# Attention read-out and three-way maxout on one Trainium2 core: two maxima apart, permuted state tokens, shared copies and new orders

## The chip, the cores and the metric

The kernel runs on one core of one Trainium2 chip, so there is no traffic between cores. The metric is the device time of one execution in microseconds (us). TensorE is called PE in the profile (its weight loads PEld), VectorE DVE, ScalarE ACT, GpSimd POOL and SyncE SP; ACT, POOL and SP also issue DMA transfers, each from its own queue.

## What is computed

There are 8 batches of 8 heads, 512 tokens and 32 state tokens per batch, and 64 numbers per head. The tokens read the states by softmax attention, and the states read the tokens. Both read-outs, 544 rows of 512 numbers per batch, then pass through three weight matrices at once; the largest of the three products is kept, and a fourth matrix gives the output.

```python
scores = scale * x @ state.T                  # 512 x 32 for a head
a = exp(scores - max); a /= a.sum(-1)
xread = a @ state                             # tokens read states
sread = softmax(scale * state @ x.T) @ x      # states read tokens
t = concatenate([xread, sread])               # 544 rows of 512 in a batch
h = maximum(maximum(t @ w1, t @ w2), t @ w3)  # 768 wide
out = h @ w_out                               # 512 wide, float32
```

## The kernel before

The kernel never forms xread. For each batch it multiplies the states into the weights first: G is state times w1, w2 and w3 (`g_slice` and `g_run`, matmuls of L326, copied out of PSUM at L344, L365 and L368). A token's row of t @ w is then its 256 attention weights times G.

A batch b passes through these steps. Each has a short name in the order strings.

- `lx`, `lxg`, `lxu` load x; `lw`, `lwo` load the weights, `lst` the states. `lw m0 m1 i` loads columns 128 m0 to 128 m1 of weight i, counted from 0. `stc`, `stt`, `stp` cast, transpose and place the states.
- `xt`/`xtc` (or `xtd`, a DMA transpose on SP's queue) give x transposed. `sc` makes the scores (L234), `ex` the exponentials on ACT (L241), `sum` their sums on DVE (L248, L250), `wt` the weights a (L256).
- `at`/`atc` (or `atd`, again a DMA transpose on SP's queue) give aT. `pad`, `sr`, `srs`, `srt` form sread and put it, transposed, into the tile `ats`.
- `g`/`gc` and `gr`/`grc` give G. Batches 0 and 1 take it in slices of 128 columns of each weight, later ones in runs of columns.
- `l1 b m` is layer 1 for slice m of the 768 columns: six matmuls of 512 columns into three PSUM banks `pw` (L378). `m0` copies the first bank to a bf16 tile t0 on ACT (L393). `m1` does two maxima on DVE, one behind the other: t1 = max(t0, second bank) at L399, and ht = max(t1, third bank) at L404.
- `l2 b j` is layer 2, six matmuls of 512 columns (L411), one for each slice m. `l2c` copies the result to the tile `osb` (L418), `so` stores it (L438).
- `l1s`, `l2 s`, `sos` do the same for the 256 state tokens of all batches at the end: twelve matmuls of 256 columns for a slice.

PSUM has four single banks (pool `pw`, which layer 1, layer 2, `sr`, the transposes and the short `gr` share) and two pairs of banks (pool `two`, for G and the scores). A matmul into a bank waits until the copy or maximum that read its last contents is done.

The order on every engine is written by hand, in three strings: FIRST (batches 0 and 1, and the start of 2), EACH (performed five times, b = 2 to 6, for layer 1 of batch b, the attention of batch b+1 and layer 2 of batch b-1) and LAST (layer 1 of batch 7, layer 2 of 6 and 7, the state tokens). `perform` (L491) walks through them, and each engine and each queue works off its part in that order. `busy n` issues n matmuls on zeros (L183), which compute nothing.

The end of the program checks sums and would branch to a slower form for other inputs; that branch doesn't run here.

Of the kernel before, what the change touches and what calls it, by code (L numbers as in the profile page):

```python
# [8 lines left out]
F32 = mybir.dt.float32  # L9
BF16 = mybir.dt.bfloat16  # L10
# [4 lines left out]


FIRST = """
    lxg 0 1; lst 1 S; lxu 0 0 A; lxg 1 0; ident; zero; busy 2; lw 0 2 1; lst 0 A; lxg 1 1; clr 0; clr 1;
    lw 0 3 0; busy 2; busy 1; busy 6; busy 1; lw 0 3 2; stc 0 P; stc 1 P; cxu 0 0 A; busy 1; busy 5; stt 0;
    busy 2; xt 0 0; busy 1; clr 3; warm; lw 2 6 1; stp 0 D; xt 0 1; xtc 0 1 D; lw 3 4 0; lw 3 4 2;  # L20
    xtc 0 0 A; xt 1 0; sc 0 0; xtc 1 0 D; ex 0 0; busy 1; sum 0 0; sc 0 1; xt 1 1; lx 2; ex 0 1; busy 2;
    sc 1 0; xtc 1 1 A; sum 0 1; stt 1; busy 2; xones 0; ex 1 0; wt 0 0 P; wt 0 1 P; sc 1 1; sum 1 0; busy 2;
    wt 1 0 P; sr 0; at 0 0; ex 1 1; at 0 1; xones 1; srs 0; stp 1 A; sum 1 1; g 0 0; wt 1 1 P; g 1 1;
    atc 0 1 A; atc 0 0 A; gc 0 0 D; sr 1; at 1 0; busy 1; srs 1; lw 4 6 2; g 0 1; g 1 0; gc 1 1 A; at 1 1;
    atc 1 1 A; gc 0 1 D; l1 0 0; g 0 2; gc 1 0 D; g 1 2; atc 1 0 A; m0 0 0; gc 0 2 A; l1 1 0; m0 1 0;
    gc 1 2 A; m1 0 0; l1 1 1; g 0 3; g 1 3; m0 1 1; m1 1 0; l1 0 1; m1 1 1; lw 4 6 0; m0 0 1; l1 0 2; xtd 2;
    l1 1 2; pad 2; m0 0 2; g 0 4; g 0 5; gc 0 3 A; gc 1 3 A; m0 1 2; gc 0 4 A; gc 0 5 A; clr 2; m1 0 1;
    l1 0 3; g 1 4; m0 0 3; lst 3 S; m1 0 2; gr 2 0 512; m1 1 2; grc 2 0 512 A; m1 0 3; l1 1 3; m0 1 3;
    sc 2 -; gc 1 4 A; l1 0 5; l1 1 4; m1 1 3; m0 0 5; lwo; l1 0 4; lst 2 S; gr 2 1024 1280; m1 0 5; g 1 5;
    m0 1 4; lx 3; ex 2 -; gr 2 1280 1792; xtd 3; m0 0 4; m1 1 4; sr 2; m1 0 4; grc 2 1024 1280 A; l2 0 2;  # L30
    sum 2 -; gc 1 5 D; l2 0 3; l2 0 0; gr 2 1792 2304; lx 4; wt 2 - P; l2c 0 3 D; stc 2 D;
    grc 2 1280 1792 A; srs 2; gr 2 512 1024; l2c 0 0 D; l2c 0 2 D; l1 1 5; m0 1 5; stt 2; grc 2 1792 2304 A;
    stc 3 P; grc 2 512 1024 A; l2 0 1; stt 3; m1 1 5; atd 2; l2c 0 1 D; stp 2 A; so 0 0 2 P; stp 3 D;
    so 0 2 4 P; ones;
"""
EACH = """
    sc 1 -; l2 -1 0; gr 1 1792 2304; gr 1 0 512; srt -2; ex 1 -; lx 3; grc 1 1792 2304 D; pad 1; l2 -1 3;
    l2c -1 0 D; l1 0 0; grc 1 0 512 A; l2 -1 1; m0 0 0; sum 1 -; l2c -1 3 A; gr 1 1024 1280; m1 0 0;
    gr 1 1280 1792; gr 1 512 1024; sr 1; grc 1 1024 1280 A; l1 0 1; l1 0 2; l2c -1 1 D; m0 0 1; srs 1;
    m0 0 2; l2 -1 2; m1 0 1; m1 0 2; grc 1 512 1024 A; l1 0 3; wt 1 - P; grc 1 1280 1792 D; m0 0 3; m1 0 3;  # L40
    l2c -1 2 A; l1 0 5; l1 0 4; xtd 2; so -1 0 2 P; m0 0 5; m0 0 4; m1 0 5; atd 1; m1 0 4; so -1 2 4 P;
"""
LAST = """
    srt 5; srt 6; l1 7 0; l2 6 2; l2 6 1; m0 7 0; l1 7 2; l2c 6 1 A; l1 7 3; l1 7 4; l2c 6 2 D; srt 7;
    m1 7 0; l1s 0; m0 7 2; m0 7 3; l1 7 1; l1 7 5; m0 7 4; m1 7 2; m0 s 0; l2 6 0; m0 7 1; m1 7 3; m1 7 4;
    l2 6 3; m1 s 0; l1s 2; l1s 1; m0 7 5; m1 7 1; m1 7 5; l2 7 0; l2 7 1; m0 s 2; l2c 6 0 D; l1s 3; look;
    m1 s 2; m0 s 1; l2p 7 2 0 256; l1s 5; l2c 6 3 D; l2c 7 0 D; m0 s 3; l2pc 7 2 0 256 A; so 6 0 2 A;
    sop 7 2 0 256 S; m1 s 1; l2c 7 1 D; m0 s 5; m1 s 3; l2p 7 2 256 512; m1 s 5; l1s 4; m0 s 4;
    l2pc 7 2 256 512 D; m1 s 4; l2 s 0; l2c s 0 D; flag; l2 7 3; sos 0 S; l2c 7 3 D; sop 7 2 256 512 S;
    so 7 3 4 S; l2 s 1; so 6 2 4 A; l2c s 1 A; so 7 0 2 P; sos 1 A;  # L50
"""


# [1 line left out]
def kernel(  # L55
# [10 lines left out]
    nc = tc.nc  # L66

    B, H, S, D = x.shape
    _, _, Ns, _ = state.shape
# [3 lines left out]
    d_model, d_ff = moe_w1.shape  # L73
# [3 lines left out]
    J = 4  # L77
    HS = H // 2
# [5 lines left out]
    data = ctx.enter_context(tc.tile_pool(name="data", bufs=1))  # L84
    work = ctx.enter_context(tc.tile_pool(name="work", bufs=2))
# [4 lines left out]
    copier = {"D": nc.vector.tensor_copy, "A": nc.scalar.copy, "P": nc.gpsimd.tensor_copy}  # L90
# [10 lines left out]
    x_f = {}  # L101
    w_sb = data.tile([128, HS, 3, d_ff], BF16, name="w")
    wout_sb = data.tile([128, NM, d_model], BF16, name="wout")
    zero = const.tile([128, 512], BF16, name="zero")
    ident = const.tile([128, 128], BF16, name="ident")
    ones = const.tile([128, 128], BF16, name="ones")
    warm = const.tile([128, 1], F32, name="warm")
    ats = data.tile([128, B, HS, Ns], BF16, name="ats")
    seen = data.tile([128, B, J * H + 2], F32, name="seen")
    flag = data.tile([128, 1], I32, name="flag")  # L110
# [32 lines left out]
        nc.gpsimd.dma_start(out=x_part(b, g), in_=x_heads(b, g))  # L143

    def load_x_uncast(b, g, q):
        x_f[b, g] = data.tile([128, HS, J * D], F32, name=f"xf{b}{g}")
        queue[q].dma_start(out=x_f[b, g], in_=x_heads(b, g))

    def cast_x(b, g, c):
# [211 lines left out]
    def g_ran(b, c0, c1, c):  # L361
        p, ps = open_ps.pop(("g", b, c0))
        v = G[b].rearrange("p g i f -> p g (i f)")[:, :, c0:c1]
        if p is not None:
            copier[c](out=v, in_=p[:, :, 0:c1 - c0])  # L365
        else:
            for g in range(2):
                copier[c[g % len(c)]](out=v[:, g], in_=ps[g][:, 0:c1 - c0])  # L368
# [3 lines left out]
    def maxout(b, m, n, lhs, rhs, nk, by_k=False):  # L372
        if m == 0 and b not in ht:
            new(ht, b, [128, NM, n], "ht" if b != "s" else "hts", bufs=4 if b != "s" else 1)
        pw = open_ps["l", b, m] = [bank([128, 512], F32, f"pw{i}") for i in range(3)]
        for i, k in [(i, k) for k in range(nk) for i in range(3)] if by_k else [
                (i, k) for i in range(3) for k in range(nk)]:
            nc.tensor.matmul(pw[i][:, 0:n], lhs(i, k), rhs(k), start=(k == 0), stop=(k == nk - 1))  # L378
# [4 lines left out]

    def layer1_states(m):
        f = slice(m * 128, m * 128 + 128)
        maxout("s", m, B * Ns, lambda i, k: w_sb[:, k, i, f], lambda k: ats[:, :, k, :], HS)

    t0s = {}

    def max_first(b, m):  # L390
        n = B * Ns if b == "s" else 512
        t0s[b, m] = work.tile([128, 512], BF16, tag="t0", bufs=3, name="t0")
        nc.scalar.copy(out=t0s[b, m][:, 0:n], in_=open_ps["l", b, m][0][:, 0:n])  # L393

    def max_rest(b, m):
        n = B * Ns if b == "s" else 512
        t0, pw = t0s.pop((b, m)), open_ps.pop(("l", b, m))
        t1 = work.tile([128, 512], BF16, tag="t1", name="t1")
        nc.vector.tensor_max(t1[:, 0:n], t0[:, 0:n], pw[1][:, 0:n])  # L399
        h, v, w = ht[b][:, m, :], t1[:, 0:n], pw[2][:, 0:n]  # L400
        if b == "s":
            h = h.rearrange("p (j n b) -> p j b n", j=2, b=4)
            v, w = [z.rearrange("p (j b n) -> p j b n", j=2, b=4) for z in (v, w)]
        nc.vector.tensor_max(h, v, w)  # L404

    def layer2(b, j):
        if b not in osb:
# [54 lines left out]
    def set_flag():  # L462
# [16 lines left out]
        "atc": (a_turned, 1), "atd": (a_turn_dma, 1), "pad": (pad, 1), "sr": (sread, 1),  # L479
        "srs": (sread_scale, 1), "srt": (sread_turn, 1), "g": (g_slice, 1), "gc": (g_sliced, 1),  # L480
        "gr": (g_run, 1), "grc": (g_ran, 1), "l1": (layer1, 1), "l1s": (layer1_states, 0),
        "m0": (max_first, 1), "m1": (max_rest, 1), "l2": (layer2, 1), "l2c": (layer2_out, 1),
        "l2p": (layer2_part, 1), "l2pc": (layer2_part_out, 1), "sop": (store_part, 1), "so": (store, 1), "sos": (store_states, 0), "look": (look_at_sums, 0), "flag": (set_flag, 0),
    }

# [69 lines left out]
    with tc.If(bad != 0, label="again"):  # L555
        for b in range(B):
            for d in (xT, e, a, aT, G, ht, osb, xp):
                d.pop(b, None)
            for g, c in ((0, "A"), (1, "D")):
                x_turn(b, g)  # L560
                x_turned(b, g, c)
            scores_below_max(b)
            sums(b)
            weights(b, None, "D")
            for g, c in ((0, "A"), (1, "D")):
                a_turn(b, g)
                a_turned(b, g, c)
            if b >= 2:
                pad(b)
            sread_below_max(b)  # L570
            sread_scale(b)
            sread_turn(b)
            for m in range(NM):
                g_slice(b, m)
                g_sliced(b, m, "A")
            for m in range(NM):
                layer1(b, m)
                max_first(b, m)
                max_rest(b, m)
            for j in range(J):  # L580
                layer2(b, j)
                layer2_out(b, j, "A")
                store(b, j, j + 1, "S")
        osb.pop("s")
        for m in range(NM):
            layer1_states(m)
            max_first("s", m)
            max_rest("s", m)
        for j in range(2):
            layer2("s", j)  # L590
            layer2_out("s", j, "A")
            store_states(j, "S")
# [30 lines left out]
```

## Time and profile before

| | us |
|---|---|
| three runs | 159.68, 159.92, 160.17 (median 159.92) |
| the profiled execution | 160.0 |
| its span, first to last event | 158.2 |
| PE busy in it | 148.6 |
| DVE busy | 121.3 |
| ACT busy | 76.1 |
| POOL busy | 53.1 |

The span is what the profiler saw of one execution; 1.8 us of that execution's time lie outside it. A row of the profile gives line, engine, operation and tiles, the number of instructions, their busy time and mean duration, and the idle time before them with what ended it. Matmuls are pipelined, so that their durations overlap: 12 matmuls of 512 columns stand in the timeline from 67.63 to 70.23 us, which is 0.216 us from one to the next, though the mean duration of one is 0.38 us. So "busy" on PE doesn't mean "at full rate".

### The profile page before, as it was taken

What the parts mean: (1) busy time and instruction counts of PE and PEld (TensorE: products, weight loads), DVE (VectorE), ACT (ScalarE), POOL (GpSimd) and SP (SyncE); (2) the same over time, 40 slices, a digit from 0 to 9 for tenths busy, and PEclk for the clock granted to TensorE, in tenths of its full rate; (3) what the DMA queues carried; (4) which work ended last, traced back from release to release, by engine and by line L of the source; (5) the groups of instructions that cost most, each with busy time, mean ns of one, the idle gap of its engine ahead of it and who ended that gap; (6) DMA issues with size and microseconds to landing.
All of it is one profiled execution on the core that took longest, in us unless ns stands there. A gap on an engine that the chain in (4) does not pass through costs nothing.

```text
span 158.2 us, 3500 instructions
## 1 busy us (share of the span) xinstructions
PE 148.6 (94%) x1384; PEld 70.9 (45%) x1384; DVE 121.3 (77%) x198; ACT 76.1 (48%) x124; POOL 53.1 (34%) x71
## 2 busy tenths in 40 slices
PE   6979999999999999999999999999999999999950
PEld 2365534434444443354344433444444445558510
DVE  4096898789989796979797979797979689767620
ACT  3259768963384645465545554555455153102010
POOL 6977737001558335334432424242321000001000
PEclk9999999999999999999999999999999999999996
DMA  4999999999889999997968940721063100002841
GB/s 135 209 192 207 190 197 157 176 206 166 172 99 320 140 196 179 215 56 198 266 89 66 253 157 2 185 91 71 0 186 112 58 0 4 0 0 110 327 171 71
DMA packets 36931, 22.28 MB, mean 141 GB/s; under 512 B 21808, under 2 KB 34608, under 8 KB 36912
## 3 DMA queue, kind: packets, MB, share of 16 engines
q0 software_dynamic: 14704, 13.90, 47.2%
q1 hardware_dynamic: 21104, 6.16, 24.2%
q10 hardware_dynamic: 1104, 1.97, 3.4%
q8 instruction: 12, 0.20, 0.5%
q14 instruction: 7, 0.06, 0.1%
HBM read 15.20 MB, written 8.91 MB: 152 GB/s over the span
## 4 chain that ended last, share of the span: by engine, by line
PE 66%; DVE 14%; DMA 6%; issue 5%; POOL 2%; ACT 2%; DVEq 0%; POOLq 0%
PE pw L378 33%; PE po L411 23%; DVE t L399 7%; DMA w<-in_moe_w_dram 6%; PE pg L326 5%; DVE ht L404 4%; PE psr L299 2%; ACT t L393 2%; POOL x L143 1%; DVE hts L404 1%; PE pgh L326 1%; POOL w L153 1%; PE po L426 1%; DVE seen L248 1%; PE ps L234 1%
## 5 line engine op out<-in xcount | busy, mean ns | idle before, releaser
L378 PE MATMUL pw<-aT,G 128*128 128x512 bf16 x288 | 67.0, 379 | 0.1
L393 ACT CAST t<-pw 128x512 bf16<-128x512 f32 (+1 forms) x54 | 30.5, 564 | 42.9 <-PE pw L378 39.5
L411 PE MATMUL po<-wout,ht 128*128 128x512 bf16 x186 | 45.1, 380 | 0.7 <-DVE ht L404 0.7
L378 PEld LDWEIGHTS <-G 128*128 128x128 bf16 x288 | 27.1, 97 | 33.7 <-issue 2.9
L399 DVE TENSOR_TENSOR t<-t,pw 128x512 bf16<-128x512 bf16 (+1 forms) x54 | 35.0, 648 | 6.7 <-ACT t L393 5.1
L404 DVE TENSOR_TENSOR ht<-t,pw 128x512 bf16<-128x512 bf16 x48 | 33.0, 687 | 5.4 <-PE pw L378 0.6
L256 POOL TENSOR_TENSOR a<-e,rden 128x1024 bf16<-128x1024 bf16 (+1 forms) x10 | 15.6, 1564 | 35.0 <-ACT osb L418 20.1
L411 PEld LDWEIGHTS <-ht 128*128 128x128 bf16 x186 | 16.9, 98 | 22.5 <-DVE ht L404 2.7
L438 POOL DMA_DIRECT2D out_dram<-osb x13 | 7.4, 569 | 52.2 <-DVE osb L418 26.8
L418 DVE COPY osb<-po 128x512 f32<-128x512 f32 x21 | 14.4, 688 | 4.2 <-PE po L411 3.3
L365 ACT CAST G<-pg 128x1024 bf16<-128x1024 f32 x14 | 14.1, 1017 | 5.2 <-PE pg L326 5.1
L365 DVE CAST G<-pg 128x1024 bf16<-128x1024 f32 x10 | 12.2, 1220 | 4.7 <-PE pg L326 4.7
L283 POOL COPY xp<-x 128x1024 bf16<-128x1024 bf16 x12 | 12.3, 1067 | 3.2 <-DMA x<-in_x_dram 3.2
L326 PE MATMUL pg<-w,bd 64*32 64x512 bf16 (+1 forms) x288 | 10.9, 362 | 0.3 <-DMA w<-in_moe_w_dram 0.3
L248 DVE TENSOR_REDUCE seen<-e 128x32 f32<-128x1024 bf16 (+1 forms) x10 | 9.9, 992 | 1.4 <-ACT e L241 1.4
L418 ACT COPY osb<-po 128x512 f32<-128x512 f32 x12 | 7.1, 591 | 7.6 <-PE po L411 7.6
L183 PE MATMUL idle<-zero 128*128 128x512 bf16 x29 | 9.4, 454 | 1.3 <-DVE zero L161 1.3
L241 ACT ACTIVATE e<-ps 128x1024 bf16<-128x1024 f32 (+1 forms) x10 | 8.4, 854 | 3.8 <-PE ps L234 2.1
L378 PE MATMUL pw<-ats,w 128*128 128x256 bf16 x72 | 9.1, 272 | 0.1
L378 PEld LDWEIGHTS <-w 128*128 128x128 bf16 x72 | 7.0, 98 | 2.0 <-issue 0.5
L368 ACT CAST G<-pgh 128x256 bf16<-128x256 f32 x12 | 3.9, 375 | 7.9 <-PE pgh L326 7.9
L326 PEld LDWEIGHTS <-bd 64*32 64x32 bf16 x336 | 3.6, 89 | 8.1 <-issue 7.4
(59 smaller groups left out, 97.9 us busy)
## 6 DMA issues: line engine op xcount, KB each, us to landing
out_dram<-osb POOLq DMA_DIRECT2D x13, 512.0 KB, 4.3
x<-in_x_dram POOLq DMA_DIRECT2D x6, 512.0 KB, 11.1
out_dram<-osb ACTq DMA_DIRECT2D x2, 512.0 KB, 3.9
x<-in_x_dram POOLq DMA_DIRECT2D x3, 256.0 KB, 6.2
w<-in_moe_w_dram POOLq DMA_DIRECT2D x3, 256.0 KB, 6.6
w<-in_moe_w_dram POOLq DMA_DIRECT2D x2, 384.0 KB, 9.0
wout<-in_moe_w_out_dram POOLq DMA_DIRECT2D x1, 768.0 KB, 10.1
xf<-in_x_dram ACTq DMA_DIRECT2D x1, 512.0 KB, 4.0
```

The lines of the kernel that those rows point to most:

```text
L183: nc.tensor.matmul(p, zero[:, 0:128], zero, start=True, stop=True)
L248: nc.vector.reduce_sum(out=den, in_=parity(e[b], g), axis=AX.X)
L256: times[c](out=parity(a[b], g).rearrange("p j g s n -> p j (g s) n"), in0=parity(e[b], g).rearrange("p j g s n -> p j (g s) n"), in1=rdens ...
L283: nc.gpsimd.tensor_copy(out=xp[b][:, :, :, g * (D + 1):g * (D + 1) + D], in_=v[:, g])
L326: nc.tensor.matmul(p(s, g), bd(b, 2 * s + g)[64 * g:64 * g + 64, g, :], f(w_sb[64 * g:64 * g + 64, s]), start=True, stop=True, tile_positi ...
L365: copier[c](out=v, in_=p[:, :, 0:c1 - c0])
L378: nc.tensor.matmul(pw[i][:, 0:n], lhs(i, k), rhs(k), start=(k == 0), stop=(k == nk - 1))
L393: nc.scalar.copy(out=t0s[b, m][:, 0:n], in_=open_ps["l", b, m][0][:, 0:n])
L399: nc.vector.tensor_max(t1[:, 0:n], t0[:, 0:n], pw[1][:, 0:n])
L404: nc.vector.tensor_max(h, v, w)
L411: nc.tensor.matmul(p, ht[b][:, m, j * 128:(j + 1) * 128], wout_sb[:, m, :], start=(m == 0), stop=(m == NM - 1))
L418: copier[c[i]](out=o[:, j, i * w:i * w + w], in_=p[:, i * w:i * w + w])
```

## The change

The diff has five parts. The order strings are shown in full for EACH and in their first lines for FIRST; LAST is described behind the diff.

1. `m1` becomes two steps, `ma` (second bank) and `mb` (third bank), and t1 has three buffers instead of two.
2. The state tokens' permutation moves. Before, `m1` wrote ht of the states in the order n, b from data in the order b, n. Now the layer-1 matmuls read `ats` in the order n, b, and the maxima are plain.
3. `gc`, `grc` and `l2c` may name two engines ("DA": DVE takes the first half and ACT the second).
4. The last tiles go out in parts: layer 2 of batch 7, j = 3, as 128, 256 and 128 columns, and more, smaller stores.
5. All three orders are arranged anew. The weights of the first slice are loaded by themselves, `xf` takes a buffer of `osb`, and 22 matmuls on zeros are left of 29.

```diff
 FIRST (first lines)
-    lxg 0 1; lst 1 S; lxu 0 0 A; lxg 1 0; ident; zero; busy 2; lw 0 2 1; lst 0 A; lxg 1 1; clr 0; clr 1;
-    lw 0 3 0; busy 2; busy 1; busy 6; busy 1; lw 0 3 2; stc 0 P; stc 1 P; cxu 0 0 A; busy 1; busy 5; stt 0;
-    busy 2; xt 0 0; busy 1; clr 3; warm; lw 2 6 1; stp 0 D; xt 0 1; xtc 0 1 D; lw 3 4 0; lw 3 4 2;
...
+    lxg 0 1; clr 0; clr 1; zero; ones; lxu 0 0 S; ident; lst 0 S; lxg 1 0; stc 0 D; busy 3; lxg 1 1;
+    lw 0 1 0; busy 10; busy 2; stt 0; xones 0; cxu 0 0 D; xt 0 0; xt 0 1; xones 1; busy 1; lw 0 2 1; warm;
+    xtc 0 0 D; stp 0 A; lst 1 S; sc 0 0; lw 0 1 2; xtc 0 1 D; busy 2; lw 1 3 0; ex 0 0; sc 0 1; ex 0 1;
+    lw 1 3 2; sum 0 0; lw 2 4 1; lw 3 6 0; xt 1 0; xt 1 1; xtc 1 0 A; stc 1 P; clr 3; lw 3 4 2; busy 1;
+    xtc 1 1 A; busy 1; sr 0; sum 0 1; sc 1 0; wt 0 0 P; srs 0; sc 1 1; wt 0 1 P; busy 1; ex 1 0; ex 1 1;
+    at 0 0; stt 1; sum 1 0; sr 1; g 1 0; g 0 0; lxg 2 0; sum 1 1; wt 1 0 P; at 0 1; wt 1 1 D; stp 1 A;
+    atc 0 0 A; gc 1 0 A; busy 1; at 1 0; at 1 1; atc 0 1 D; g 1 1; g 0 1; gc 0 0 AD; gc 1 1 A; l1 0 0;
...
 EACH
-    sc 1 -; l2 -1 0; gr 1 1792 2304; gr 1 0 512; srt -2; ex 1 -; lx 3; grc 1 1792 2304 D; pad 1; l2 -1 3;
-    l2c -1 0 D; l1 0 0; grc 1 0 512 A; l2 -1 1; m0 0 0; sum 1 -; l2c -1 3 A; gr 1 1024 1280; m1 0 0;
-    gr 1 1280 1792; gr 1 512 1024; sr 1; grc 1 1024 1280 A; l1 0 1; l1 0 2; l2c -1 1 D; m0 0 1; srs 1;
-    m0 0 2; l2 -1 2; m1 0 1; m1 0 2; grc 1 512 1024 A; l1 0 3; wt 1 - P; grc 1 1280 1792 D; m0 0 3; m1 0 3;
-    l2c -1 2 A; l1 0 5; l1 0 4; xtd 2; so -1 0 2 P; m0 0 5; m0 0 4; m1 0 5; atd 1; m1 0 4; so -1 2 4 P;
+    gr 1 1792 2304; gr 1 0 512; grc 1 0 512 A; l2 -1 3; sc 1 -; ex 1 -; l2c -1 3 AD; l2 -1 0; l2 -1 1;
+    grc 1 1792 2304 A; sum 1 -; l1 0 0; gr 1 512 1024; gr 1 1024 1280; pad 1; l2c -1 0 A; m0 0 0;
+    gr 1 1280 1792; sr 1; l2c -1 1 D; grc 1 1024 1280 A; ma 0 0; l1 0 1; xtd 2; mb 0 0; l1 0 2; srt -2;
+    srs 1; wt 1 - P; m0 0 1; l1 0 3; so -1 0 2 P; m0 0 2; m0 0 3; grc 1 1280 1792 DA; ma 0 1; l1 0 5;
+    l2 -1 2; m0 0 5; grc 1 512 1024 A; mb 0 1; ma 0 2; mb 0 2; ma 0 3; l1 0 4; mb 0 3; ma 0 5; l2c -1 2 DA;
+    mb 0 5; lx 3; m0 0 4; ma 0 4; so -1 2 4 A; atd 1; mb 0 4;

 def load_x_uncast(b, g, q):
-        x_f[b, g] = data.tile([128, HS, J * D], F32, name=f"xf{b}{g}")
+        o = work.tile([128, J, d_model], F32, tag="osb", bufs=3, name="osb")
+        x_f[b, g] = o.rearrange("p j f -> p (j f)")[:, 0:HS * J * D].rearrange("p (s jd) -> p s jd", s=HS)

 def g_ran(b, c0, c1, c):
-            copier[c](out=v, in_=p[:, :, 0:c1 - c0])
+            for g, h in ((0, 2),) if len(c) == 1 else ((0, 1), (1, 2)):
+                copier[c[g]](out=v[:, g:h], in_=p[:, g:h, 0:c1 - c0])

 def layer1_states(m):
-        maxout("s", m, B * Ns, lambda i, k: w_sb[:, k, i, f], lambda k: ats[:, :, k, :], HS)
+        maxout("s", m, B * Ns, lambda i, k: w_sb[:, k, i, f],
+               lambda k: ats[:, :, k, :].rearrange("p (j b) n -> p j n b", b=4), HS)

-    def max_rest(b, m):
...
-        t1 = work.tile([128, 512], BF16, tag="t1", name="t1")
-        nc.vector.tensor_max(t1[:, 0:n], t0[:, 0:n], pw[1][:, 0:n])
...
-            h = h.rearrange("p (j n b) -> p j b n", j=2, b=4)
...
-        nc.vector.tensor_max(h, v, w)
+    def max_second(b, m):
...
+        t1s[b, m] = work.tile([128, 512], BF16, tag="t1", bufs=3, name="t1")
+        nc.vector.tensor_max(t1s[b, m][:, 0:n], t0s.pop((b, m))[:, 0:n], open_ps["l", b, m][1][:, 0:n])
+
+    def max_third(b, m):
...
+        nc.vector.tensor_max(ht[b][:, m, :], t1s.pop((b, m))[:, 0:n], open_ps.pop(("l", b, m))[2][:, 0:n])
```

In `ats` two neighbours b of one n lie 128 bf16 elements, 256 bytes, apart; two neighbours n of one b lie side by side. The matmul of the changed kernel steps through b first, four at a time.

LAST keeps its set of matmuls but for the parts of 7 3. It ends, as before, with layer 2 of the states (`l2 s 0`, `flag`, `l2 s 1`), their copies and their stores; the last copy is now shared by ACT and DVE, and the stores of batches 6 and 7 in LAST are 11 smaller ones instead of 6, on POOL's, ACT's and SP's queues.

## The prediction, written before the changed kernel had run

> **What bounds the kernel now.** I read the page's busy times and slices first, then the chain of waits, then groups with shapes, then single stretches of the timeline.
>
> ```profile
> span 158.2 us, 3500 instructions
> ...
> PE   6979999999999999999999999999999999999950
> ...
> DVE  4096898789989796979797979797979689767620
> ACT  3259768963384645465545554555455153102010
> ...
> PEclk9999999999999999999999999999999999999996
> ```
>
> PE is busy from the fourth slice to 152 us at full granted clock; DVE is close behind in the middle, and ACT and DMA have room there. So three things can be won: the start before PE has real work, time that PE loses inside its busy row, and the end behind its last matmul. The chain in order of time shows the first:
>
> ```profile
> 5.05 0.71 POOL w L153
> 5.76 9.61 DMA w<-in_moe_w_dram
> 15.37 0.14 issue
> 15.51 0.52 PE pg L326 x16
> 16.03 0.63 PE psr L299 x32
> ...
> 18.08 1.29 PE pw L378 x6
> ```
>
> The first G waits until 15.4 us for weights, layer 1 begins at 18.0 (17.92 in the timeline). For the second I take a stretch of PE's timeline of one pass through EACH:
>
> ```profile
> 70.23 1.46 PE L411 MATMUL po<-wout,ht 128*128 128x512 bf16 x6
> 71.52 4.08 PE L378 MATMUL pw<-aT,G 128*128 128x512 bf16 x18
> 75.44 0.63 PE L234 MATMUL ps<-bd,xT 128*128 128x64 bf16 x16
> 75.90 1.03 PE L411 MATMUL po<-wout,ht 128*128 128x512 bf16 x4
> 77.11 0.60 PE L411 MATMUL po<-wout,ht 128*128 128x512 bf16 x2 [0.18 <-DVE ht L404]
> 77.64 0.63 PE L326 MATMUL pg<-w,bd 64*32 64x512 bf16 x16
> ```
>
> 18 matmuls take 3.92 us from start to start, 0.216 each, but the six of layer 2 from 75.90 to 77.64 take 1.74 instead of 1.30: the last maximum of layer 1 comes late, 0.44 us lost. A pass at the rate of its own rows would be 60 matmuls x 0.216 = 12.96, plus 0.55 and 0.67 for G, 0.38 for sr, 0.46 for the scores: 15.02. It takes, from one `l1 b 1` to the next in the chain (52.09, 67.69, 83.31, 99.24, 114.91), 15.60, 15.62, 15.93 and 15.67.
>
> **The sum is made against the profiled execution,** 160.0 us, which is 0.08 above the median of 159.92. What comes after 152.3 counts as it is: copy 0.59, then 5.3 to the end of the span.
>
> **Start.** PE can't start layer 1 before G of slices 0 and 1 and aT of both batches are there. As bf16, 256+384+384 KB of weights stand ahead of the first G before, 128+256+128 after. DMA moves 192 to 209 GB/s in these slices, so the first G's weights land 524 KB / 200 = 2.6 us sooner, at 12.8. But slice 1 needs two loads of 256 KB more, which makes the same 1024 KB as before: 15.4 still. The attention of batch 1 becomes the later gate. The second half of its x no longer queues behind 256 KB of weights: 11.5 - 1.3 = 10.2. PE has 15 matmuls on zeros first, and they start about 0.9 later (two memsets of 0.49 go ahead of `zero`): the states are turned at about 7.4 (before 7.2), exponentials of batch 0 come at 9.8 (before 10.0). From there by rows: transposes of x to 11.3, their ACT copies (1.01 each) to 13.0, scores 0.41, exponentials (0.60) to 14.2, sum 0.68 and reciprocal 0.25 to 15.5 (DVE has 15.0 to 16.1 now). The weights of that half move from POOL (1.05) to DVE. DVE has no such row; between 0.4 (the 256-wide maximum) and 1.05 (POOL's) I take 0.65, the 512-wide maximum. Then transpose, two G of 0.5, copies (DVE 0.42 to 0.5 each): layer 1 at about 17.0 instead of 17.92, **-0.9** (-0.2 to -1.6). Casting x of batch 0 on DVE, 1.05 on ACT before, has bounds of 0.8 (DVE's 512-wide cast) and 1.6 (twice that); it is hidden by the matmuls on zeros up to 7.4.
>
> From there to layer 2 of batch 0 PE needs 11 slices x 1.30 + G 1.94 + 0.88 + scores 0.46 + sr 0.38 = 17.9, and took 18.96 (17.92 to 36.88). The 1.05 are bank waits on ACT and DVE; the new order gives ACT two and a half more of the twelve G copies (0.80 each), and it was busy 15 of 20 us. I take half of the loss back: **-0.5** (0 to -1.0). Two gates cap it: x of batch 2 lands behind the same bytes (22.15, transposed 8.0 later: 30.15, wanted at 30.4), and wout lands at 24.17 + 10.1 = 34.3, wanted at 34.9. Past these the start can't gain more than 36.88 - 34.3 = 2.6.
>
> **The passes of EACH.** PE's work is the same 15.02. What moves is what it waits for. Per pass DVE had two G copies of 1.22, two copies of 0.68, sums 1.56, sr 0.46, twelve maxima of 0.69: 14.1, and has now one half copy of about 0.68, one copy of 0.68, two halves of 0.45: 12.6. ACT goes from 8.4 to 10.2 plus a DMA issue of 0.4, of 15.4; it has room. PE now ends a pass with slices 1, 2, 3, 5, then `l2 2`, then slice 4, and runs two G and five sixths of `l2 3` before it needs the last maximum. I set the rows one behind the other from the start of a pass. sr ends at 7.3, but slice 1 waits for `mb 0` of slice 0, at 7.6: 0.3 lost. DVE then does sr (0.46), the half G copy and five pairs (1.40 a pair, as 68.89 to 70.29 before), with its half of `l2c 2` in between, and slice 4's last bank is free when PE comes, because it waits for ACT's half, not for `mb 5`. PE ends at 15.4, `mb 4` at 16.8, and the sixth matmul of `l2 3` wants it at 17.0. So 15.4 a pass, four times: 62.82 - 61.6 = 1.2; I take **-1.0** (0 to -2.2, the whole loss). The cover is thin, 0.2 us: a pair that takes 0.05 more costs it, and then every pass loses up to 0.3 again.
>
> **End.** The states' third maximum writes in order now:
>
> ```profile
> L404 DVE TENSOR_TENSOR hts<-t,pw 128x256 bf16<-128x256 bf16 x6 | 4.4, 730 | 0.6
> ...
> L399 DVE TENSOR_TENSOR t<-t,pw 128x256 bf16<-128x256 bf16 x6 | 2.5, 417 | 1.8 <-PE pw L378 1.1 <-ACT t L393 0.7
> ```
>
> Six times 0.73 to 0.42 is 1.9 us of DVE, where DVE is at 75%: it counts only where PE waits for it. From 114.91 to 152.32 PE needs 36.4 (36 slices and tiles of 1.30 for layers 1 and 2, some in parts, six of 1.31 for the states) and took 37.4. Of the 1.0 lost I take 0.5 back; the parts of 128 columns cost 12 x 0.07 (transposes of 128 columns: 16 in 1.16) against 6 x 0.11, +0.2; the shared last copy takes 0.45 instead of 0.59, -0.14. More stores are issued earlier; the last one leaves as before. **-0.4** (-1.1 to +0.6).
>
> **The price that no row shows** is the matmul that reads `ats` in steps of 256 bytes. 72 matmuls of 256 columns come every 0.109 us (12 in 1.31). Below nothing isn't possible: PE reads the same number of columns. The nearest row is DVE's permuted maximum: 0.31 us more for 256 elements, which about doubles the price of an element (0.69 - 0.42 = 0.27 for 256 plain ones). If PE paid double likewise: 72 x 0.107 = +7.7, all on its path, since PE has no gaps there. I take 0, because a matmul's weights and results don't change and every other PE row of this trace keeps the same 0.42 ns a column whatever tile it reads; but none of them reads with a step.
>
> [...]
>
> **Sum:** 160.0 - 0.9 - 0.5 - 1.0 - 0.4 = **157.2**. A difference of 0.3% is about what a measurement of this kernel can tell from no change.
>
> **Rivals.**
> - *The permuted read halves PE's rate* in the state slices: 157.2 + 7.7 = 164.9. For it: DVE's row. Against it: nothing measured, only that PE isn't DVE. It decides from +2.8, a price of 0.039 us a matmul, on.
> - *New waits take the place of the old ones:* the start is held by the attention of batch 1, DVE's pairs are a little slower than taken, and a pass loses the 0.4 elsewhere. For it: DVE 80% busy, spare times of 0.2 to 0.6. Start -0.3, passes -0.3, end -0.2: 159.2.
> - *The orders fit fully:* PE loses nothing from 17.0 on, -0.9 - 1.05 - 2.2 - 0.9 = 155.0. Against it: the wait at slice 1 and the caps above.
>
> **Chances.** Forecast (155.5 to 158.6) 0.60; all fits 0.10; waits swap 0.14, of which 0.07 still faster, 0.06 the same, 0.01 slower; permuted read 0.13; other slowdowns (a DMA that is late at one of the two caps) 0.03. So faster 0.77, same 0.06, slower 0.17. The range 154.9 to 159.6 leaves out the two slow cases and a little of the fast one; the far end of the permuted read, 164.9, lies outside it with its 0.13.
>
> **What would show it.** First weights at about 12.8 and layer 1 at 17.0 in the chain; layer 2 of batch 0 at 35 to 35.5; 15.4 us between passes with no idle of PE on ht; `pw<-ats,w` 12 in 1.31 as before (2.6 if the rival holds); hts maxima at 0.42; 5.3 us from the last copy to the end. I am wrong if these matmuls slow down, if ACT's row fills in the first 20 us, or if a pass is still 15.6.

## The result, and the profile after

The changed kernel takes 190.8 us (median of 4 runs, 189.82 to 192.11) beside 160.04 for the kernel before on the same chip: a ratio of 1.193 (95% interval 1.185 to 1.201), 31 us slower. The prediction was 157.2, with 154.9 to 159.6 as its range. The profiled execution took 190.81, with a span of 188.9.

The page of the changed kernel, busy times and the span in 40 slices (4.7 us each):

```profile
span 188.9 us, 3541 instructions
...
PE   5998998999999999999999999999999999999980
...
DVE  2588996998887488498658748875534103422110
...
PEclk9999999999999999999999999999969756955567
```

PE is busy to the end, as before, and DVE runs empty in the last quarter. So PE itself has more to do there, or does it more slowly; no engine keeps it waiting. The last row says a second thing: from the 30th slice on the granted clock is down to half for long stretches. Before, it was full (9 in the row, 90% or more) up to PE's last matmul. The groups, with shapes apart, name the place (count, then busy time and mean ns of one). The first row is that of the kernel before, the others are those of the changed kernel:

```profile
L378 PE MATMUL pw<-ats,w 128*128 128x256 bf16 x72 | 9.1, 272 | 0.1
```

```profile
L385 PE MATMUL pw<-ats,w 128*128 128x256 bf16 x72 | 32.1, 611 | 0.0
...
L411 DVE TENSOR_TENSOR hts<-t,pw 128x256 bf16<-128x256 bf16 x6 | 2.5, 421 | 5.9 <-PE pw L385 5.9
```

The maxima of the states went to 0.42 us as foreseen. The 72 matmuls that read `ats` have a mean of 611 ns instead of 272. Matmuls overlap, so I read the rate from start to start in PE's timeline:

```profile
133.88 5.37 PE L385 MATMUL pw<-ats,w 128*128 128x256 bf16 x12
139.07 4.16 PE L385 MATMUL pw<-aT,G 128*128 128x512 bf16 x12
143.07 2.33 PE L385 MATMUL pw<-ats,w 128*128 128x256 bf16 x5
```

Twelve matmuls of a state slice take 139.07 - 133.88 = 5.19 us instead of 1.31: 0.4325 each instead of 0.109, four times. Six slices: 6 x 3.88 = 23.3 us. The second row is as telling: twelve plain matmuls of 512 columns, which read nothing with a step, take 4.00 instead of 2.59. For these the clock is to blame: at 0.50 from 139.07 to 141.94 it costs them 1.43, by an estimate from these times. The windows below are cut where the clock changes, found with windows of 0.2 us (columns: busy time of each engine, granted clock, DMA share, GB/s):

```profile
135.00:138.40 3.40, 3.40 (x9) 0.92 (x8) 0.86 (x2) 0.37 (x1) 0.00 (x0) 1.00 0.00 0
138.80:141.70 2.90, 2.90 (x9) 0.95 (x7) 1.06 (x2) 0.58 (x1) 0.00 (x0) 0.50 0.01 3
...
149.00:158.80 9.80, 9.80 (x24) 3.14 (x23) 0.45 (x1) 0.96 (x2) 1.07 (x2) 0.50 0.20 80
...
166.20:182.60 16.40, 16.40 (x45) 5.39 (x43) 3.16 (x10) 1.70 (x4) 0.00 (x0) 0.50 0.12 41
```

PE's busy share is full in each, and the clock is 1.00 or 0.50 (1.00 in the two rows left out). By these small windows it changes at 138.53, 141.94, 148.77, 159.01, 165.84 and 182.90. The stretches between are 3.41, 6.83, 10.24, 6.83 and 17.06 us: one, two, three, two and five times 3.41. It fell at the end of such a period of 3.41 us when the stepped matmuls had filled 2.9 us of it (to 148.77) or all of it (to 138.53 and 165.84); after 2.3 us (from 143.07 to 145.35) it stayed. It came back after a period that held mostly plain ones (0.54 us of stepped ones in the one to 141.94, none in those to 159.01 and 182.90).

Two smaller losses lie ahead of this. A pass of EACH, from one `psr` to the next, takes 16.04, 15.98, 16.05 and 16.05 us (before 15.61, 15.61, 15.93 and 15.67; predicted 15.4). PE's timeline shows where:

```profile
99.67 0.45 PE L305 MATMUL psr<-xp,e 128*32 128x65 bf16 x32
100.46 5.36 PE L385 MATMUL pw<-aT,G 128*128 128x512 bf16 x24 [0.34 <-DVE ht L411]
...
106.95 1.68 PE L385 MATMUL pw<-aT,G 128*128 128x512 bf16 x6
108.56 0.62 PE L332 MATMUL pg<-w,bd 64*32 64x512 bf16 x16
```

sr to slice 1 takes 0.79 instead of 0.38, since slice 1 waits for the last maximum of slice 0, and slice 4 takes 1.61 instead of 1.30. And in the start, the chain of waits goes through x of batch 2:

```profile
14.26 0.99 POOL a L262
15.25 7.38 DMA x<-in_x_dram
...
22.71 9.01 DMA xT<-x
...
31.76 0.64 PE ps L240 x16
```

Layer 1 begins at 17.21, near the 17.0 that I had put, but PE then waits 0.64 us for the transposed x (the last row's own duration is by chance the same). Its second half is issued only at 15.25, behind twelve transfers and three multiplications on POOL; before, one transfer of all of it was issued at 9.81.

### The profile page after: what moved, and what is told of

Same layout as the page of the kernel before. It is cut to its first block, busy times and chain, and to the rows that moved or that the text cites. A ratio compares the mean times of both kernels' runs of the same rounds, so it can differ in the third digit from the quotient of the medians.

```text
span 188.9 us, 3541 instructions
## 1 busy us (share of the span) xinstructions
PE 176.6 (93%) x1389; PEld 74.5 (39%) x1389; DVE 113.9 (60%) x207; ACT 83.3 (44%) x142; POOL 53.6 (28%) x72
## 4 chain that ended last, share of the span: by engine, by line
PE 66%; DVE 9%; DMA 9%; POOL 6%; issue 4%; ACT 3%; DVEq 0%; ACTq 0%; POOLq 0%; SPq 0%
PE pw L385 39%; PE po L418 21%; DMA xT<-x 5%; DMA x<-in_x_dram 4%; POOL w L159 3%; DVE osb L425 2%; DVE ht L411 2%; PE pg L332 2%; DVE t L407 2%; DVE seen L254 2%; PE ps L240 2%; PE po L433 2%; POOL a L262 2%; ACT osb L425 2%; ACT e L247 1%
## 5 line engine op out<-in xcount | busy, mean ns | idle before, releaser
L385 PE MATMUL pw<-aT,G 128*128 128x512 bf16 x288 | 68.8, 385 | 2.3 <-DVE ht L411 1.7
L385 PE MATMUL pw<-ats,w 128*128 128x256 bf16 x72 | 32.1, 611 | 0.0
L425 DVE COPY osb<-po 128x256 f32<-128x256 f32 (+1 forms) x24 | 12.5, 519 | 27.0 <-PE po L418 13.9
L372 ACT CAST G<-pg 128x1024 bf16<-128x1024 f32 (+1 forms) x23 | 20.4, 890 | 4.7 <-PE pg L332 4.3
L425 ACT COPY osb<-po 128x256 f32<-128x256 f32 (+1 forms) x22 | 9.9, 456 | 19.0 <-DVE osb L425 7.9
L445 POOL DMA_DIRECT2D out_dram<-osb x9 | 5.2, 579 | 39.3 <-ACT osb L425 35.9
L350 ACT CAST G<-pg 128x768 bf16<-128x768 f32 (+1 forms) x12 | 8.5, 724 | 4.4 <-PE pg L332 3.2
L189 PE MATMUL idle<-zero 128*128 128x512 bf16 x22 | 7.2, 461 | 2.4 <-DVE zero L167 2.4
L159 POOL DMA_DIRECT2D w<-in_moe_w_dram x10 | 7.7, 782 | 0.0
L148 POOL DMA_DIRECT2D x<-in_x_dram x9 | 7.1, 796 | 0.9 <-POOLq L616 0.9
```

The costliest lines, as they stand in the source:

```text
L159: nc.gpsimd.dma_start(out=w_sb[:, :, i, m0 * 128:m1 * 128], in_=(moe_w1, moe_w2, moe_w3)[i].rearrange("(kk p) f -> p kk f", p=128)[:, :, m ...
L372: copier[c[g]](out=v[:, g:h], in_=p[:, g:h, 0:c1 - c0])
L425: copier[c[i]](out=o[:, j, i * w:i * w + w], in_=p[:, i * w:i * w + w])
```

## Experiments

**Theory:** the read of `ats` in steps of 256 bytes makes each column four times as dear, and the slow matmuls cost the clock as well; the rest of the change loses a few us more. **Rival:** the new orders, parts and shared copies are the loss, and the read is dear only beside them. The first runs are two that undo or do the one part.

```diff
 plain read: the changed kernel with
-               lambda k: ats[:, :, k, :].rearrange("p (j b) n -> p j n b", b=4), HS)
+               lambda k: ats[:, :, k, :], HS)
 and the third maximum of the states in the order n, b again
 only permuted: the kernel before with that line the other way round, and plain maxima
```

> The changed kernel with one part undone: layer 1 of the state tokens reads the tile ats in the plain order b, n again, and the third maximum of the states writes in the order n, b as before. Theory (the stepped read of ats is the loss): the twelve matmuls of a state slice come back from 5.19 us to 1.31, which is 6 x 3.88 = 23.3 us, and the some 6 us that other matmuls lost in the last 55 us beside a granted clock of 0.5 to 0.9 come back too, so 190.8 - 29 = about 161 (160 to 163), with the granted clock at 0.99 or more throughout. Rival A (the clock falls for another reason, such as the new order of LAST): only the 23.3 come back, 167 or more, with the clock still below 0.9 behind 134 us. Rival B (orders, parts and shared copies are the loss): 175 or more.

> The kernel before with one part of the change alone: layer 1 of the state tokens reads ats in the order n, b, and the maxima of the states are plain. Theory: 160.0 + 23.3 for 72 matmuls at 0.4325 instead of 0.109 us, and up to 6 more if the granted clock falls as it did in the changed kernel: 183 to 190. Rival (the slow matmuls need the new order of LAST, where the state slices stand between others): within 3 us of 160.

Measured: **plain read 163.2 us** (ratio to before 1.022, 1.018 to 1.026), granted clock 0.998; **only permuted 187.7 us** (1.178, 1.173 to 1.183). The read alone costs 187.7 - 159.7 = 28.0, and taking it out of the changed kernel gives back 190.8 - 163.2 = 27.6. Of these, at the rates above, 23.3 are the 72 matmuls, whose row in the only-permuted kernel is the one of the changed kernel:

```profile
L378 PE MATMUL pw<-ats,w 128*128 128x256 bf16 x72 | 32.1, 612 | 0.0
```

The rest is plain matmuls at half clock. Set beside the kernel before, row by row from the first state slice to the end of the span, the only-permuted kernel takes 22.9 us more for the state slices (23.3 less 0.5 of waits that slices of before still held), 5.8 more for the plain matmuls between and behind them, and 0.7 less behind the start of the last six: 28.0. In that run the clock changes at 134.9, 138.3, 145.2, 155.4, 162.2 and 179.3, again in multiples of 3.4. So the rival falls: the read needs no new order to be dear. But 3.5 us remain that it doesn't explain.

**What the price hangs on.** Three runs put other reads of 256 columns into the six slices of the kernel before; the third also moves where some of them begin.

```diff
-        maxout("s", m, B * Ns, lambda i, k: w_sb[:, k, i, f], lambda k: ats[:, :, k, :], HS)
+        v = ats.rearrange("p b k n -> p (b k n)")
+        q = (pattern of slice m, as (step, count) pairs in elements)
+        maxout("s", m, B * Ns, lambda i, k: w_sb[:, k, i, f], lambda k: bass.AP(v.tensor, v.offset, (v.ap[0],) + q), HS)
```

> The kernel before, in which the six state slices read their 256 columns in different steps: every 2nd element (4 bytes), every 4th (8 bytes), steps of 16, 32 and 64 bytes, and runs of 4 elements (8 bytes) that lie 32 bytes apart. The rows of the state tokens are then not the reference's. Theory A (a column that opens a new 16-byte line costs more): steps of 4 and 8 bytes cost little (0.109 us a matmul, up to 0.2), 16, 32 and 64 bytes all about 0.43; runs of 4 about 0.19. Theory B (any step other than the neighbouring element costs the full price): all of 4, 8, 16, 32, 64 bytes take 0.43, and runs of 4 between 0.19 and 0.43. Theory C (the price grows with the distance): it rises from step to step and reaches 0.43 only at 64 bytes or beyond.

> The kernel before again, with six more ways to read 256 columns of ats, in the order in which the slices run: every 4th element (8 bytes, two columns in each 16-byte line) at full clock; runs of two neighbours 16 bytes apart; the eight elements of each line in the order 0, 4, 1, 5, 2, 6, 3, 7; runs of four 32 bytes apart; plain; and columns that go to and fro between two neighbouring lines. The rows of the state tokens are not the reference's. Theory A (PE's read brings one 16-byte line in about 1.69 ns, 0.4325 us by 256, and a matmul takes the longer of this and 0.42 ns a column): 0.216, 0.216, 0.109, 0.109, 0.109 and 0.43 us a matmul. Theory B (a step that isn't the neighbour costs the full 1.69 ns): 0.43, 0.27, 0.43, 0.19, 0.109 and 0.43.

> The kernel before once more with other reads of ats (the rows of the state tokens are not the reference's), to test a rule that was made after the two earlier runs with steps: PE takes the columns of the moving operand four at a time, a group of four takes 1.69 ns for every 16-byte line that it touches, or 0.42 ns a column if that is longer. In the order in which the slices run: plain, begun 2 elements behind a line's start (every other group touches two lines, and three lines fall to two groups); plain, begun 1 element behind (the same); every 2nd element, begun 4 elements behind (every group touches two lines); runs of four that cross a line, 32 bytes apart (two lines a group); every 3rd element (two lines in each group); and columns that go round four neighbouring lines (four lines a group). By the rule: 0.163, 0.163, 0.216, 0.216, 0.216 and 0.433 us a matmul at full clock. Rival (only the step counts, not where the read begins): 0.109, 0.109, 0.116, 0.115, between 0.116 and 0.226, and 0.226 to 0.433. The granted clock should stay at 1.0 through the first five by the rule, since none of these slices reaches a quarter of the rate, and at most fall in the last.

From PE's timeline of the three (a slice lasts to the start of the next row; a row of 24 is two slices back to back). The first, with 16 bytes and then 8 in the row of 24, then 32 and 64 bytes:

```profile
136.69 8.30 PE L378 MATMUL pw<-ats,w 128*128 128x256 bf16 x24
144.81 2.89 PE L413 MATMUL po<-wout,ht 128*128 128x512 bf16 x12
147.54 5.68 PE L378 MATMUL pw<-ats,w 128*128 128x256 bf16 x12
153.04 1.46 PE L428 MATMUL po<-wout,ht 128*128 128x256 bf16 x6
...
156.81 5.33 PE L378 MATMUL pw<-ats,w 128*128 128x256 bf16 x12
161.96 2.58 PE L413 MATMUL po<-wout,hts 128*128 128x512 bf16 x6
```

The second, with 8 bytes and, at the end, to and fro between two lines:

```profile
129.99 2.89 PE L378 MATMUL pw<-ats,w 128*128 128x256 bf16 x12
132.70 2.77 PE L378 MATMUL pw<-aT,G 128*128 128x512 bf16 x12
...
148.62 3.08 PE L378 MATMUL pw<-ats,w 128*128 128x256 bf16 x12
151.53 1.59 PE L413 MATMUL po<-wout,hts 128*128 128x512 bf16 x6
```

The third:

```profile
130.90 1.54 PE L378 MATMUL pw<-ats,w 128*128 128x256 bf16 x12
132.27 2.98 PE L378 MATMUL pw<-aT,G 128*128 128x512 bf16 x12
...
137.68 3.08 PE L378 MATMUL pw<-ats,w 128*128 128x256 bf16 x24
140.60 2.75 PE L413 MATMUL po<-wout,ht 128*128 128x512 bf16 x12
143.19 2.89 PE L378 MATMUL pw<-ats,w 128*128 128x256 bf16 x12
145.90 0.84 PE L428 MATMUL po<-wout,ht 128*128 128x256 bf16 x6
146.57 2.23 PE L378 MATMUL pw<-ats,w 128*128 128x256 bf16 x12
148.63 0.82 PE L428 MATMUL po<-wout,ht 128*128 128x256 bf16 x6
149.29 5.44 PE L378 MATMUL pw<-ats,w 128*128 128x256 bf16 x12
154.56 2.43 PE L413 MATMUL po<-wout,hts 128*128 128x512 bf16 x5
```

All three runs together, each slice at full clock but where said:

| read of 256 columns | changes of 16-byte line | us a matmul |
|---|---|---|
| plain; plain, begun 2 elements behind | 32, 33 | 0.109, 0.114 |
| the eight elements of a line in the order 0, 4, 1, 5, ... | 32 | 0.109, but for one wait of 0.11 in the slice |
| every 2nd element (4 bytes) | 64 | 0.116 |
| runs of four, 32 bytes apart | 64 | 0.115 |
| every 3rd element (6 bytes) | 96 | 0.172 |
| every 4th element (8 bytes) | 128 | 0.226 |
| runs of two, 16 bytes apart | 128 | about 0.226 |
| runs of four that cross a line | 128 | 0.226 |
| steps of 16, 32, 64, 256 bytes | 256 | 0.45, 0.46, 0.43, 0.4325 |
| round four neighbouring lines | 256 | 0.44 |
| to and fro between two neighbouring lines | 256 | 0.243 |

(The 0.114 of the shifted plain read is that of its place: the kernel before takes 0.114 there too, since one matmul of the slice waits. In the first run the slice with steps of 8 bytes fell to half clock, where a plain one takes 0.21 too, by an estimate from six of 512 columns in 2.53 us, from 178.39 in the changed kernel, so its figure is from the second; the slice with 32 bytes ended at half clock.) The 16 bytes are read from the table: a step of 16 costs what a step of 256 costs (0.45 and 0.4325), a step of 8 half of it (0.226). 0.4325 us by 256 is 1.69 ns, and every row but the last is, to within 8%, the longer of 1.69 ns for a change of line and 0.42 ns for a column. So theory A of the first two runs holds, B and C fall. The rule about groups of four, which I made to explain the last row, fell in its own test: with it a plain read that begins off a line's start should take 0.163, and the 24 matmuls from 137.68 some 4.5 us; they took 2.92, where the plain ones of before take 2.88. The last row stays unexplained.

The granted clock agrees: through five slices at half the rate or more it stayed at 1.0, though none of those at half the rate lasted over 2.8 us, so none filled a period of 3.41 us. Only behind the sixth, which took 3.05 of the 3.41 us before it, it fell, at 154.9, for 3.4 us.

**The other 3.5 us.** With the plain read, each of the three new orders was put alone between the old ones.

```diff
 first only: FIRST of the changed kernel, EACH and LAST of before (m1 b m written as ma b m; mb b m)
 each only:  EACH of the changed kernel, FIRST and LAST of before
 last only:  LAST of the changed kernel, FIRST and EACH of before
```

The three keep the other parts of the change, such as the third buffer of t1 and `xf` in a buffer of `osb`.

> Plain read of ats; the order of the changed kernel in FIRST alone, with the orders of before in EACH and LAST. The run with the plain read and all three new orders took 163.2 us beside 159.7 before, 3.4 more. Theory (each order loses what the trace shows: the start gains 0.7 on layer 1 and gives it back to the wait for x of batch 2, a pass loses 0.35 five times, LAST nothing): 160 to 160.8. Rival (the start alone holds the loss, through DMAs that are late for the passes): 162 or more. Rival (the start keeps its gain once the passes are the old ones): 158.5 to 159.3.

> Plain read of ats; the order of the changed kernel in EACH alone, with the orders of before in FIRST and LAST. Theory (five passes of 16.0 instead of 15.65): 161.2 to 162. Rival (a pass is as long as what FIRST leaves behind makes it, and in steady state it takes 15.4 as I had put it): 158.5 to 159.5.

> Plain read of ats; the order of the changed kernel in LAST alone, with the orders of before in FIRST and EACH. Theory (parts, smaller stores and the new order of LAST change nothing that ends last): 159.3 to 160.2. Rival (LAST holds a good part of the 3.4): 160.8 or more. Rival (the -0.4 of the prediction holds): 159.2 or less.

Measured, beside 159.69 for before: **FIRST 161.3** (ratio 1.012, 1.009 to 1.015), **EACH 162.6** (1.019, 1.016 to 1.022), **LAST 160.1** (1.003, 1.001 to 1.005). Each of the three loses, also the LAST that I had put at a small gain. Their sum, 5.0, is more than the 3.5 of all three together: a new order beside an old one has waits of its own at the seam (the new FIRST lets the old EACH wait 0.46 us before 48.8 us, for a transpose of a). So these are bounds on what each order costs rather than shares. EACH alone has passes of 15.99, 15.98, 16.24 and 16.05, FIRST alone of 15.66, 15.61, 15.69 and 15.68: the longer pass belongs to EACH's own order.

**Shared copies.** In the trace the two halves of a shared copy don't run side by side. The row of DVE in the changed kernel that copies its half of `l2c 3` waits for ACT's half:

```profile
112.53 0.42 DVE L425 COPY osb<-po 128x256 f32<-128x256 f32 x1 [2.54 <-ACT osb L425]
112.87 1.21 DVE L254 TENSOR_REDUCE seen<-e 128x32 f32<-128x1024 bf16 x1
```

ACT gets to its half only behind the exponentials, and DVE's sums stand behind DVE's half.

```diff
 unshared: plain read, all new orders, and in EACH
-l2c -1 3 AD; ... grc 1 1280 1792 DA; ... l2c -1 2 DA;
+l2c -1 3 A; ... grc 1 1280 1792 D; ... l2c -1 2 A;
```

> As the run with the plain read, and in EACH the three shared copies are done by one engine each (layer 2 of j = 3 and j = 2 on ACT, the G run 1280 to 1792 on DVE). Theory (two engines that copy halves of one tile go one behind the other, so that sharing delays the second half and what is queued behind it): a pass of EACH takes 15.4 to 15.8 us instead of the 16.0 of the run with the plain read, and the whole is 1 to 2 us faster than it. Rival (sharing costs nothing, the pass is longer because of the order of PE): the pass stays at 15.9 to 16.1 and the time within 0.5 us of the run with the plain read.

Measured: 162.6 us (1.020, 1.016 to 1.024) beside 163.2 for the plain read, and passes of 16.11, 15.99, 16.00 and 16.00. The theory fell as stated: the passes are the rival's, and the 0.6 us that the whole gained lie just outside what either allowed. The sums did start earlier, and slice 4 lost 0.09 instead of 0.31; but G's copy on DVE alone held DVE 0.5 us longer, and slices 1 and 2 lost 0.40 for it. The wait of slice 1 was hardly touched (0.35 instead of 0.41), since the maximum ahead of it (`ma 0`) now waited for ACT's copy of slice 0's first bank instead of the sums. That pointed to the place itself: the first bank of slice 1 is the one that slice 0's last maximum frees. In the order of before, layer 2 of j = 1 lies between and takes the turn. The next run mends this, and gives only the copies of layer 2 to one engine each.

```diff
 each mended: plain read, FIRST and LAST of before, EACH of the changed kernel with
-l2c -1 3 AD; l2 -1 0; l2 -1 1; grc 1 1792 2304 A; sum 1 -; l1 0 0; gr 1 512 1024; gr 1 1024 1280; pad 1; l2c -1 0 A; m0 0 0;
-gr 1 1280 1792; sr 1; l2c -1 1 D; grc 1 1024 1280 A; ma 0 0; l1 0 1; xtd 2; mb 0 0; l1 0 2; ... l2c -1 2 DA;
+l2c -1 3 D; l2 -1 0; l1 0 0; l2c -1 0 A; m0 0 0; l2 -1 1; grc 1 1792 2304 A; sum 1 -; ma 0 0; mb 0 0; gr 1 512 1024; gr 1 1024 1280;
+pad 1; l2c -1 1 A; gr 1 1280 1792; sr 1; grc 1 1024 1280 A; l1 0 1; xtd 2; l1 0 2; ... l2c -1 2 A;
```

> Plain read of ats, the orders of before in FIRST and LAST, and in EACH the order of the changed kernel with two things mended: layer 1 of slice 0 goes ahead of layer 2 of j = 1, so that the sr tile and not slice 1 takes the bank of slice 0's last maximum, which follows the sums at once; and the copies of layer 2 are done by one engine each (j = 3 on DVE, the others on ACT). Theory (0.41 us of a pass were the wait of slice 1 for that maximum, 0.2 the shared copy of j = 2 that holds slice 4's last bank): a pass of 15.3 to 15.5 instead of 16.0, and 157.9 to 159.0. Rival A (only the copy mattered): 15.7 to 15.8 a pass, 160 to 161. Rival B (DVE is late either way and the wait only moves): 16.0 a pass, 162.6.

Measured: **158.8 us** (9 runs, 158.21 to 159.33), ratio 0.992 (0.989 to 0.995), **0.8% below the kernel before, and below the changed one**. Passes of 15.29, 15.28, 15.29 and 15.28, at the lower end of what the theory put:

```profile
67.04 0.45 PE L301 MATMUL psr<-xp,e 128*32 128x65 bf16 x32
67.42 5.38 PE L381 MATMUL pw<-aT,G 128*128 128x512 bf16 x24
...
73.93 1.46 PE L381 MATMUL pw<-aT,G 128*128 128x512 bf16 x6
75.32 0.63 PE L328 MATMUL pg<-w,bd 64*32 64x512 bf16 x16
```

sr takes its 0.38, slice 1 waits for nothing, slice 4 takes 1.39. Of the 0.31 at slice 4, 0.09 is the step to G, which is still there. So 0.41 and 0.22 are gone, and 0.13 ahead of sr (0.46 from the start of the last eight matmuls of G to sr in the changed kernel, 0.33 here): 0.76, and a pass of 16.05 became one of 15.29. All were mended in one run, so their shares are read from the trace alone. What PE still loses are steps of 0.09 where the 64*32 tiles of G follow full 128*128 tiles: six matmuls take 1.39 instead of 1.30 up to them, from 64.98 to 66.37 and from 73.93 to 75.32.

**The start.** The last of the three orders mends x of batch 2.

```diff
 first mended: as first only, with
-lw 3 6 0; ... lw 3 4 2; ... lxg 2 0; ... lxg 2 1;
+lw 3 6 0; ... lx 2; ... lw 3 4 2; ...
```

> As the run with the new FIRST alone (161.3 us), but x of batch 2 is loaded in one transfer, issued on POOL's queue ahead of the weights of slice 3's third matrix and of the multiplications by the reciprocals, as before. Theory (POOL issues x of batch 2 at 13.5 and 15.3 us instead of 9.8, so that scores of batch 2 wait 0.72 us for its transpose and everything behind it is later): the wait goes and the time falls by 0.6 to 1.2, to 160.1 to 160.7. Rival (the wait is covered by the bank waits that follow it): 161.0 or more.

Measured: 161.5 us (1.010, 1.004 to 1.017), nothing gained. The wait of 0.72 is gone, but in this run layer 1 begins at 18.20 instead of 17.29, and bank waits take back more than half of the gain: from layer 1 to layer 2 of batch 0 it is 19.02 instead of 19.32. The rival holds. From the start of layer 1 to sr of the first pass of EACH, PE takes 33.72 us before, 35.44 with the new FIRST and 35.14 here. So the new FIRST loses its time behind the start of layer 1, in waits for x of batch 2, for a transposed a and for banks; which change of its order makes them is left open.

**The permutation in the store.** If neither the read nor the maxima permute, the store could place the rows.

```diff
 store plain: the kernel before, plain maxima, and in store_states
-            out=out.rearrange("(b t) f -> b t f", t=SP)[4 * j:4 * j + 4, S:SP, :].rearrange("b n f -> n b f"),
+            out=out.rearrange("(b t) f -> b t f", t=SP)[4 * j:4 * j + 4, S:SP, :],
```

> The kernel before without any permutation inside the core: the states' maxima are plain, ats is read plainly, and the store of the states' rows writes them to their places in the order b, n (each of 128 partitions holds one row of 2 KB either way). Theory (the permutation can be left to the store for nothing, and 6 x 0.31 us of DVE go, of which PE waited for 0.3 to 0.6): 159.1 to 159.5 beside 159.7. Rival (stores in this order take longer at the end, where nothing hides them): 160.3 or more.

Measured: 164.8 us (1.031, 1.025 to 1.037). The last copy begins 0.5 us earlier, as the theory said, but its end is followed by 10.7 us instead of 5.3:

```profile
151.83 0.59 ACT L415 COPY osb<-po 128x512 f32<-128x512 f32 x1 [4.59 <-PE po L408]
```

From 155 to 160 us the DMA engines of this run move 55 to 94 GB/s, where the kernel before moves 199 to 369 from 152 to 155 and is done by 156. The DMA share in these five microseconds is 0.16 to 0.30. An estimate from the share is that about four of the 16 DMA engines worked; why no more did, no run shows. The order n, b thus pays for itself in the store, and the maxima of 0.73 were the cheapest place for it that these runs found.

## Why the prediction was wrong, step by step

- **The permuted read, taken at 0 with bounds of 0 to +7.7: the step that failed.** It cost 27.6 to 28.0 us, with the clock that it took along. I reasoned that every PE row keeps 0.42 ns a column "whatever tile it reads", and noted that none of them reads with a step; that was no ground for 0. The upper bound failed too: DVE's permuted row about doubles its price, and I took that as the worst for PE. PE reads a column in 0.42 ns where DVE's plain 256-wide row takes 0.42 us, 1.6 ns an element, so a fixed price weighs four times as much on PE. Carried over as it stood and not as a factor, DVE's 0.31 us for 256 elements would have given 72 x 0.31 = 22.3 us, close to the 23.3; whether the two prices have one cause no run shows. I had put the rival at 164.9 with a chance of 0.13; its mechanism was right and its size a third.
- **The clock** wasn't in the prediction at all; every estimate assumed 1.00. It cost 5.8 us of plain matmuls. While PE had work, the clock fell at a busy share of 99 to 100% in the profile, at the ends of periods of 3.41 us; why it does no run shows.
- **Start, -0.9 for layer 1:** it began at 17.21, 17.97, 17.62 and 17.29 in the four traces with the new FIRST as it was (mean 17.52), and at 17.23 to 17.92 in the nine with the old one (mean 17.59). No gain; the one trace of before that I had was at the late end. The steps held in part: the first G, at 13.9, no longer waits for weights, and batch 1's attention is the later gate (the transpose at 15.38 waits for POOL's weights). But DVE's multiplication took 1.25 us, not 0.65. **-0.5 for bank waits:** with the new FIRST as it was there are waits of 0.22 to 1.11 us for x of batch 2 (0 to 0.61 with the old one), and layer 2 of batch 0 came at 36.4 to 37.7, not 35 to 35.5. I had named x of batch 2 as a cap, but took its landing from the bytes in front of it and not from the issues on POOL, which now come later by 3.6 and 5.5 us (13.45 and 15.27 in the run with the new FIRST alone, against 9.81).
- **Passes, -1.0:** they became longer by some 0.4 each. The wait of slice 1, put at 0.3, measured 0.41. The second, 0.22 of the 0.31 at slice 4, came from a shared copy that I had let run on two engines at once ("it waits for ACT's half", but ACT's half waits for DVE's). And 15.02 for PE's work left out the steps of 0.09. The far bound of -2.2 wasn't "the whole loss" by its own rows: 62.82 - 4 x 15.02 is 2.74.
- **End, -0.4:** LAST alone costs +0.4 (0.2 to 0.9). The shared last copy takes 0.83, one half behind the other (ACT at 183.41, DVE from 183.82 to 184.24 in the changed kernel), not 0.45 instead of 0.59. From its end to the end of the span it is 4.7 us, not 5.3.
- **The maxima** took 0.42, as put. What they bring is seen in the run that permutes in the store: the last copy 0.5 us earlier, as much as I had taken for it. But the permutation then has to go to the read or to the store, and either costs ten times as much or more.
- **The other rivals:** without the stepped read the kernel takes 163.2, above even "new waits take the place of the old ones" (159.2). Its mechanism is what happened, on all three orders, and larger than I had put it.

## What to carry to other kernels

Look at the innermost order in which a matmul's moving operand is read before anything else: fewer than four bf16 columns in a row from the same 16 bytes slowed PE down in every pattern here, from 0.109 us a matmul to 0.172 at about three, 0.226 at two and 0.43 to 0.46 at one (0.243 in one pattern), and periods of 3.41 us with 2.8 us or more of matmuls at a quarter of the rate also took half of the clock from the matmuls behind them. A price that no row shows should be bounded by the fastest engine that it can stall, and an operand read 18 times is the worst place for a permutation that costs 1.9 us of DVE at the writer. When an order is arranged anew, follow each PSUM bank to who frees it last, and don't count a copy shared by two engines as half as long.

## What the runs showed of the hardware beyond the forecast

- 256 changes of 16-byte line in the moving operand made a matmul of 256 columns 0.43 to 0.46 us long, 128 of them 0.226, 96 of them 0.172, and 64 or fewer 0.109 to 0.116: the longer of 1.69 ns a change and 0.42 ns a column, to within 8%. The price didn't follow the granted clock: a stepped slice took 5.19 us at clock 1.00 (from 143.07 in the changed kernel) and 5.22 at 0.50 (from 173.17).
- Going to and fro between two neighbouring lines took 0.243 us a matmul, where as many changes of line took 0.43 or more in the other patterns. No run here tells why.
- The times between changes of the granted clock were 3.41 us, or two, three or five times that. With PE busy to 99 or 100%, it fell from 1.00 to 0.50 after periods with 2.84 us or more of matmuls at a quarter of the rate (2.84 in the only-permuted kernel, up to 162.2) and stayed at 1.00 after one with 2.36 (there, up to 158.8). Through slices at half of the rate, 2.7 us each in the second and third run with other reads, it stayed at 1.00, but none of them filled a period.
- In every pair of the changed kernel's trace, two engines that copied halves of one PSUM tile went one behind the other; where the second engine was waiting for it, it began 0.03 to 0.04 us after the first had ended. No run tells whether the chip asks for this or only the waits that the program sets.
- The order of rows in the stores of the state tokens, each of 128 rows of 2 KB, changed the time behind the last copy from 5.3 to 10.7 us.
